# GroupNorm on one core: VectorE's loop holds one tile a trip with register addresses, and the last store is cut into quarters

## The chip, the cores and the metric

One core of one Trainium2 chip. The metric is the device time of one execution, in microseconds.

## The reference

x is (128, 1024, 32, 16) in bf16. Every batch entry has 32 groups of 32 channels; each group is normalised over its 16,384 values, then scaled and shifted by channel.

```python
def reference(x, g, b):
    G = 32
    B, C, H, W = x.shape[0], x.shape[1], x.shape[2], x.shape[3]
    xr = x.reshape(B, G, C // G, H, W)
    mu = xr.mean(axis=(2, 3, 4), keepdims=True)
    var = ((xr - mu) ** 2).mean(axis=(2, 3, 4), keepdims=True)
    xn = (xr - mu) / jnp.sqrt(var + 1e-5)
    xn = xn.reshape(B, C, H, W)
    return xn * g[None, :, None, None] + b[None, :, None, None]
```

134 MB must be read and 134 MB written.

## The kernel before

A tile is four batch entries: 128 partitions (4 entries x 32 groups), 16,384 bf16 values each, 4 MB in all. There are 32 tiles and a ring of six slots in which tiles are normalised in place. The steps of a tile:

- TensorE sums 12 chunks of 512 columns with an identity matrix. VectorE adds the other 10,240 columns in pairs (`pair`, 5120 wide, with an accumulator).
- ScalarE makes the mean of both, then two Square passes with accumulators (`ja`), variance and square root.
- VectorE makes scale and bias, and 32 passes of 128x512, one a channel.
- The store leaves when the whole tile is normalised.

One queue (SyncE) issues all loads and stores: two stores at first, then always three loads and three stores. VectorE does the pair sum of the next tile before it normalises the present one. Five trips of six unrolled tiles are a loop; the last two tiles are code behind it. In the very last tile TensorE sums all 32 chunks, so VectorE has no pair sum to do.

```python
    def on_sync(e):
        def load(j):
            if j >= SLOTS:
                e.wait_ge(st[j % SLOTS], 16 * (j // SLOTS))
            e.dma_start(out=slot(j), in_=x_v[j]).then_inc(ld[j % SLOTS], 16)

        def store(i):
            e.wait_ge(done[i % SLOTS], i // SLOTS + 1)
            e.dma_start(out=o_v[i], in_=slot(i)).then_inc(
                st[i % SLOTS] if i + SLOTS < NT else s_fin, 16
            )
        for j in range(SLOTS):
            load(j)
        for i in range(NT):
            store(i)
            if i % RUN == FIRST_RUN - 1:
                for j in range(max(SLOTS, i + 1 + SLOTS - RUN), min(i + 1 + SLOTS, NT)):
                    load(j)
        e.wait_ge(s_fin, 16 * SLOTS)

    def in_rounds(e, one):
        with nc.Fori(0, TRIPS, 1, engines=[e.engine]) as t:      # TRIPS = 5, SLOTS = 6
            for c in range(SLOTS):
                one(c, t + 1)
        for c in range(NT - LOOPED):                             # the last two tiles
            one(c, TRIPS + 1)
    # ... (cut: PE, ACT)
    def on_vector(e):
        # ... (cut)
        def one(c, turn):
            follows = not isinstance(turn, int)
            then = (c + 1) % SLOTS, turn + (c + 1) // SLOTS
            if follows:
                pair(*then)
            e.wait_ge(stded[c], turn)
            # ... (cut: reciprocal, scl, bia, each behind a semaphore)
            for k in range(KC):                                  # KC = 32
                if k == 1 and follows:
                    e.wait_ge(paired[then[0]], then[1])
                a = slot(c)[:, k * HW : (k + 1) * HW]
                ts = e.tensor_scalar(
                    out=a, in0=a, scalar1=scl[:, k : k + 1], scalar2=bia[:, k : k + 1],
                    op0=ALU.mult, op1=ALU.add,
                )
            ts.then_inc(done[c], 1)
```

Of the kernel before, what the change touches and what calls it, by code (L numbers as in the profile page):

```python
# [8 lines left out]
ALU = mybir.AluOpType  # L9
# [5 lines left out]
EPS = 1e-5  # L15

SLOTS = 6
TRIPS = 5
RUN = 3
FIRST_RUN = 2  # L20
PS_BUFS = 3
PE_CHUNKS = 12
MM_FREE = 512
# [3 lines left out]
def kernel(  # L27
# [23 lines left out]
    F = KC * HW  # L51
    inv_n = 1.0 / float(F)
    NMM = F // MM_FREE
    LOOPED = TRIPS * SLOTS
    PAIRED = F - PE_CHUNKS * MM_FREE
    assert SLOTS < NT and LOOPED < NT - 1 and NT - LOOPED <= SLOTS
    assert F % MM_FREE == 0 and PAIRED % 2 == 0 and SLOTS % PS_BUFS == 0

    x_v = x.rearrange("(t n) (g k) h w -> t (n g) (k h w)", n=NS, g=G)
# [30 lines left out]
    def sem(name):  # L90
        return nc.alloc_semaphore(name)

    def sems(name):
        return [sem(f"{name}{c}") for c in range(SLOTS)]

    ld, st, summed, paired, meaned, stded, done = (
        sems(n) for n in ("ld", "st", "sum", "pair", "mean", "std", "done")
    )

    half, both, varred, inverted, scaled, shifted = (  # L100
        sems(n) for n in ("half", "both", "var", "inv", "scl", "bia")
    )
    s_gb, s_ones, s_eye, s_gbp, s_fin = (
        sem(n) for n in ("gbl", "ones", "eye", "gbp", "fin")
    )

    def slot(i):
        return ring[:, (i % SLOTS) * F : (i % SLOTS + 1) * F]
# [4 lines left out]
    def sums_and_pairs(c):  # L113
        return ps[:, c % PS_BUFS * 2 * MM_FREE : c % PS_BUFS * 2 * MM_FREE + MM_FREE + 1]

    def pairs(c):
        return ps[:, (c % PS_BUFS * 2 + 1) * MM_FREE : (c % PS_BUFS * 2 + 1) * MM_FREE + 1]

    def on_sync(e):
        def load(j):  # L120
            if j >= SLOTS:
                e.wait_ge(st[j % SLOTS], 16 * (j // SLOTS))
            e.dma_start(out=slot(j), in_=x_v[j]).then_inc(ld[j % SLOTS], 16)  # L123

        def store(i):
            e.wait_ge(done[i % SLOTS], i // SLOTS + 1)
            e.dma_start(out=o_v[i], in_=slot(i)).then_inc(
                st[i % SLOTS] if i + SLOTS < NT else s_fin, 16
            )

        for j in range(SLOTS):
            load(j)
        for i in range(NT):
            store(i)
            if i % RUN == FIRST_RUN - 1:
                for j in range(max(SLOTS, i + 1 + SLOTS - RUN), min(i + 1 + SLOTS, NT)):
                    load(j)
        e.wait_ge(s_fin, 16 * SLOTS)

    def on_gpsimd(e):  # L140
        e.wait_ge(s_ones, 1)
        e.affine_select(  # L142
            out=eye[:], in_=ones_b[:], pattern=[[-1, P]], compare_op=ALU.is_equal,
            fill=0.0, base=0, channel_multiplier=1,
        ).then_inc(s_eye, 1)
        e.affine_select(  # L146
            out=rep[:].rearrange("q (n a) -> q n a", n=NS),
            in_=ones_b[0:G, :].rearrange("q (n a) -> q n a", n=NS),
            pattern=[[0, NS], [-1, G]], compare_op=ALU.is_equal,
            fill=0.0, base=0, channel_multiplier=1,  # L150
        ).then_inc(s_eye, 1)

    def in_rounds(e, one):

        with nc.Fori(0, TRIPS, 1, engines=[e.engine]) as t:
            for c in range(SLOTS):
                one(c, t + 1)
        for c in range(NT - LOOPED):
            one(c, TRIPS + 1)

    def is_last(c, turn):
        return isinstance(turn, int) and LOOPED + c == NT - 1

    def on_tensor(e):
        e.wait_ge(s_eye, 2)
        e.wait_ge(s_gb, 32)
        e.matmul(out=gb_p[:], lhsT=rep[:], rhs=gb_b[:], start=True, stop=True).then_inc(s_gbp, 1)  # L167
        def one(c, turn):
            e.wait_ge(meaned[(c - PS_BUFS) % SLOTS], turn)
            e.wait_ge(ld[c], turn * 16)  # L170
            chunks = NMM if is_last(c, turn) else PE_CHUNKS
            for k in range(chunks):
                mm = e.matmul(  # L173
                    out=sums(c),
                    lhsT=eye[:],
                    rhs=slot(c)[:, k * MM_FREE : (k + 1) * MM_FREE],
                    start=(k == 0),
                    stop=(k == chunks - 1),
                )
            mm.then_inc(summed[c], 1)  # L180

        in_rounds(e, one)

    def on_scalar(e):
        e.dma_start(out=gb_b[:, 0:KC], in_=g_v).then_inc(s_gb, 16)
        e.dma_start(out=gb_b[:, KC : 2 * KC], in_=b_v).then_inc(s_gb, 16)
        e.wait_ge(s_ones, 1)
        e.activation(out=warm[:], in_=eps_t[:], func=ACT.Sqrt)  # L188

        def one(c, turn):  # L190
            if not is_last(c, turn):
                e.wait_ge(paired[c], turn)
            e.wait_ge(summed[c], turn)
            src = sums(c) if is_last(c, turn) else sums_and_pairs(c)
            e.activation(  # L195
                out=jm[:, 0 : src.shape[1]], in_=src, func=ACT.Identity, scale=-inv_n,
                accum_out=nm[:, c : c + 1], saturate=False,
            ).then_inc(meaned[c], 1)
            e.wait_ge(meaned[c], turn + (1 if c >= PS_BUFS else 0))
            for h in range(2):  # L200
                if h == 1:
                    e.wait_ge(half[c], turn)
                e.activation(  # L203
                    out=ja[:],
                    in_=slot(c)[:, h * (F // 2) : (h + 1) * (F // 2)],
                    func=ACT.Square,
                    bias=nm[:, c : c + 1],
                    scale=1.0,
                    accum_out=sq[:, h : h + 1],
                    saturate=False,  # L210
                ).then_inc(both[c] if h == 1 else half[c], 1)
            e.wait_ge(both[c], turn)
            e.activation(  # L213
                out=var[:], in_=sq[:, 0:1], func=ACT.Identity, bias=eps_t[:], scale=inv_n
            ).then_inc(varred[c], 1)
            e.wait_ge(varred[c], turn)
            e.activation(  # L217
                out=std[:, c : c + 1], in_=sq[:, 1:2], func=ACT.Sqrt, bias=var[:], scale=inv_n
            ).then_inc(stded[c], 1)

        in_rounds(e, one)

    def on_vector(e):
        e.memset(ones_b[:], 1.0)  # L224
        e.memset(eps_t[:], EPS)
        e.drain()  # L226
        e.sem_inc(s_ones, 1)
        for c in range(PS_BUFS, SLOTS):
            e.sem_inc(meaned[c], 1)
        e.wait_ge(s_gbp, 1)  # L230
        e.tensor_copy(out=gb[:], in_=gb_p[:])  # L231

        def pair(c, turn):
            first, w = PE_CHUNKS * MM_FREE, PAIRED // 2
            e.wait_ge(ld[c], turn * 16)
            e.scalar_tensor_tensor(  # L236
                out=jp[:],
                in0=slot(c)[:, first : first + w],
                scalar=1.0,
                in1=slot(c)[:, first + w : first + 2 * w],  # L240
                op0=ALU.mult,
                op1=ALU.add,
                accum_out=pairs(c),
                saturate=False,
            ).then_inc(paired[c], 1)

        def one(c, turn):
            follows = not isinstance(turn, int)
            then = (c + 1) % SLOTS, turn + (c + 1) // SLOTS
            if follows:  # L250
                pair(*then)
            e.wait_ge(stded[c], turn)
            e.reciprocal(out=rstd[:], in_=std[:, c : c + 1]).then_inc(inverted[c], 1)  # L253
            e.wait_ge(inverted[c], turn)
            e.tensor_scalar(  # L255
                out=scl[:], in0=gb[:, 0:KC], scalar1=rstd[:], scalar2=None, op0=ALU.mult
            ).then_inc(scaled[c], 1)
            e.wait_ge(scaled[c], turn)
            e.scalar_tensor_tensor(  # L259
                out=bia[:], in0=scl[:], scalar=nm[:, c : c + 1], in1=gb[:, KC : 2 * KC],  # L260
                op0=ALU.mult, op1=ALU.add,
            ).then_inc(shifted[c], 1)
            e.wait_ge(shifted[c], turn)
            for k in range(KC):
                if k == 1 and follows:
                    e.wait_ge(paired[then[0]], then[1])
                a = slot(c)[:, k * HW : (k + 1) * HW]
                ts = e.tensor_scalar(  # L268
                    out=a, in0=a, scalar1=scl[:, k : k + 1], scalar2=bia[:, k : k + 1],
                    op0=ALU.mult, op1=ALU.add,  # L270
                )
            ts.then_inc(done[c], 1)

        pair(0, 1)
        e.drain()  # L275
        in_rounds(e, one)

    with tc.tile_critical(no_gpsimd_drain=True):  # L278
        on_sync(nc.sync)
# [34 lines left out]
```

## Time and profile before

| | before |
|---|---|
| time, median of 4 runs | 632.68 us (632.24 to 633.53) |
| span of the profiled execution | 630.3 us |
| moved by DMA | 268.4 MB, 433 GB/s in most slices |
| VectorE, one tile | 16.56 us (95.70 to 112.26 below) |
| ScalarE, one tile | 15.75 us (504.0 / 32) |
| DMA, load and store of one tile | 19.4 us (2 x 9.7) |

The page (the profile's summary) of the kernel before, in which PE is TensorE, PEld its weight loads, DVE VectorE, ACT ScalarE and POOL GpSimd: busy shares, then the span in 40 slices (each digit the busy share in tenths).

```profile
span 630.3 us, 2508 instructions
...
PE 157.6 (25%) x405; PEld 52.0 (8%) x405; DVE 522.3 (83%) x1185; ACT 504.0 (80%) x258; POOL 0.8 (0%) x6
...
DVE  1579999999996998599589949994997799499671
ACT  0799999999996999399859958993999399769930
...
DMA  8999999999999999999999999999999999999996
GB/s 366 433 431 416 433 433 434 430 433 435 435 435 433 430 433 433 435 433 435 433 433 428 433 433 426 433 433 437 430 433 433 433 428 433 433 433 429 433 410 285
...
```

The two bottom lines matter: the DMA engines are full from the second slice to the last but one, at 430 to 435 GB/s in most of them (410 to 437 in all), while VectorE (83%) and ScalarE (80%) have slack. The slices tell two more things: the transfers start almost at once (8 in the first slice), and something is missing in the last two (410 and 285 GB/s).

VectorE in two tiles early in the kernel (start, duration, engine, line, operation, count):

```profile
...
95.70 5.50 DVE L236 SCALAR_TENSOR_TENSOR jp<-ring 128x5120 fp8e5<-128x5120 bf16 x1
...
101.91 10.42 DVE L268 TENSOR_SCALAR ring<-ring,scl,bia 128x512 bf16<-128x512 bf16 x32
112.26 5.48 DVE L236 SCALAR_TENSOR_TENSOR jp<-ring 128x5120 fp8e5<-128x5120 bf16 x1
...
```

From one pair sum to the next are 112.26 - 95.70 = 16.56 us, with no pause.

Who VectorE waits for (total us, times, longest):

```profile
...
DVE jp L236 <- DMA ring<-in_x_dram: 63.8, 9, 8.9
...
DVE rstd L253 <- ACT std L217: 15.5, 3, 6.2
...
```

Nine waits for a load, one for every three tiles: VectorE is ahead of the transfers.

The end of the kernel before, by stretches: busy us and number of instructions of PE, PEld, DVE, ACT and POOL, then the granted TensorE clock; the two last columns are the mean busy share of the 16 DMA engines and their GB/s:

```profile
...
605.00:613.00 8.00, 0.00 (x0) 0.00 (x0) 7.76 (x25) 0.10 (x1) 0.00 (x0) 0.50 1.02 442
613.00:617.00 4.00, 0.00 (x0) 0.00 (x0) 3.33 (x11) 0.00 (x0) 0.00 (x0) 0.50 0.29 123
617.00:620.00 3.00, 0.00 (x0) 0.00 (x0) 0.00 (x0) 0.00 (x0) 0.00 (x0) 0.50 1.18 502
620.00:625.00 5.00, 0.00 (x0) 0.00 (x0) 0.00 (x0) 0.00 (x0) 0.00 (x0) 0.50 0.99 426
625.00:632.00 7.00, 0.00 (x0) 0.00 (x0) 0.00 (x0) 0.00 (x0) 0.00 (x0) 0.50 0.21 90
...
```

From 613 to 617 us the DMA engines are 29% busy: VectorE is at work on the last tile (its last pass ends at 616.3 us) and only then does its store leave. This looks like 3 us to be had. But the mean hides the engines. The trace has the times of 16 landings for each transfer (increments of its semaphore), which are read here as one from each DMA engine when its share is done. In order of time (us from the span's start, taken from the trace's landing events; first, twelfth and the last four of the 16):

```
store of the last tile but one   613.87 ... 615.49   616.65  618.01  618.87  619.41
store of the last tile           627.29 ... 627.41   627.44  627.67  628.54  629.08
```

If the last landing of each belongs to the same engine, that engine took 629.08 - 619.41 = 9.67 us for its share, as long as for the transfer before (609.74 to 619.41): it never waited for VectorE. The span ends 1.3 us after it.

### The profile page before, as it was taken

What the parts mean: (1) busy time and instruction counts of PE and PEld (TensorE: products, weight loads), DVE (VectorE), ACT (ScalarE), POOL (GpSimd) and SP (SyncE); (2) the same over time, 40 slices, a digit from 0 to 9 for tenths busy, and PEclk for the clock granted to TensorE, in tenths of its full rate; (3) what the DMA queues carried; (4) which work ended last, traced back from release to release, by engine and by line L of the source; (5) the groups of instructions that cost most, each with busy time, mean ns of one, the idle gap of its engine ahead of it and who ended that gap; (6) DMA issues with size and microseconds to landing.
All of it is one profiled execution on the core that took longest, in us unless ns stands there. A gap on an engine that the chain in (4) does not pass through costs nothing.

```text
span 630.3 us, 2508 instructions
## 1 busy us (share of the span) xinstructions
PE 157.6 (25%) x405; PEld 52.0 (8%) x405; DVE 522.3 (83%) x1185; ACT 504.0 (80%) x258; POOL 0.8 (0%) x6
## 2 busy tenths in 40 slices
PE   1453205005302320250052015203510450065000
PEld 0110001001100100010010001001100110012000
DVE  1579999999996998599589949994997799499671
ACT  0799999999996999399859958993999399769930
POOL 0000000000000000000000000000000000000000
PEclk9867656556655665665566556655665665567555
DMA  8999999999999999999999999999999999999996
GB/s 366 433 431 416 433 433 434 430 433 435 435 435 433 430 433 433 435 433 435 433 433 428 433 433 426 433 433 437 430 433 433 433 428 433 433 433 429 433 410 285
DMA packets 9316, 268.48 MB, mean 426 GB/s; under 512 B 1120, under 2 KB 1120, under 8 KB 1120
## 3 DMA queue, kind: packets, MB, share of 16 engines
q1 hardware_dynamic: 9216, 268.44, 99.0%
q8 instruction: 1, 0.02, 0.0%
q14 instruction: 3, 0.02, 0.0%
q10 hardware_dynamic: 96, 0.00, 0.0%
HBM read 134.22 MB, written 134.22 MB: 426 GB/s over the span
## 4 chain that ended last, share of the span: by engine, by line
DMA 63%; DVE 26%; ACT 7%; issue 0%; SPq 0%; DVEq 0%
DMA out_dram<-ring 43%; DMA ring<-in_x_dram 20%; DVE ring L268 16%; DVE jp L236 9%; ACT ja L203 7%; DVE bia L259 0%; DVE scl L255 0%; ACT jm L195 0%; SPq L123 0%; ACT var L213 0%; DVE rstd L253 0%; ACT std L217 0%; DVEq L275 0%; SPq L309 0%; SPq L278 0%
## 5 line engine op out<-in xcount | busy, mean ns | idle before, releaser
L203 ACT ACTIVATE ja<-ring,nm 128x8192 fp8e5<-128x8192 bf16 x64 | 455.9, 7123 | 2.1
L268 DVE TENSOR_SCALAR ring<-ring,scl,bia 128x512 bf16<-128x512 bf16 x1024 | 333.7, 408 | 1.2
L173 PE MATMUL ps<-ring,eye 128*128 128x512 bf16 x404 | 157.4, 571 | 411.8 <-DMA ring<-in_x_dram 411.8
L236 DVE SCALAR_TENSOR_TENSOR jp<-ring 128x5120 fp8e5<-128x5120 bf16 x31 | 170.1, 5488 | 63.8 <-DMA ring<-in_x_dram 63.8
L195 ACT ACTIVATE jm<-ps 128x513 fp8e5<-128x513 f32 (+1 forms) x32 | 19.2, 601 | 95.0 <-DVE jp L236 95.0
L173 PEld LDWEIGHTS ps<-ring,eye 128*128 128x128 bf16 x404 | 51.9, 134 | 516.9 <-issue 467.2
L253 DVE RECIPROCAL rstd<-std 128x1 f32<-128x1 f32 x32 | 6.3, 198 | 15.5 <-ACT std L217 15.5
L203 ACT ACTIVATION_READ_ACCUMULATOR ja<-ring,nm 128x1 f32 x64 | 12.0, 187 | 0.0
L217 ACT ACTIVATE std<-sq,var 128x1 f32<-128x1 f32 x32 | 9.4, 295 | 1.0
L213 ACT ACTIVATE var<-sq,eps_t 128x1 f32<-128x1 f32 x32 | 9.4, 295 | 1.0
L259 DVE SCALAR_TENSOR_TENSOR bia<-scl,nm,gb 128x32 f32<-128x32 f32 x32 | 8.0, 251 | 1.1
L255 DVE TENSOR_SCALAR scl<-gb,rstd 128x32 f32<-128x32 f32 x32 | 7.7, 241 | 1.1
L231 DVE COPY gb<-gb_p 128x64 f32<-128x64 f32 x1 | 0.2, 225 | 10.1 <-PE gb_p L167 10.1
L195 ACT ACTIVATION_READ_ACCUMULATOR jm<-ps 128x1 f32 x32 | 6.2, 194 | 0.0
L236 DVE DVE_READ_ACCUMULATOR jp<-ring 128x1 f32 x31 | 4.4, 143 | 0.0
L167 PE MATMUL gb_p<-gb_b,rep 32*128 32x64 bf16 x1 | 0.2, 205 | 11.2 <-DMA gb_b<-in_b_dram 11.2
L188 ACT ACT_TABLE_LOAD x1 | 1.3, 1283 | 1.9 <-issue 1.9
L224 DVE MEMSET ones_b<- 128x128 bf16 x1 | 0.2, 165 | 1.1 <-SPq L278 1.1
L167 PEld LDWEIGHTS gb_p<-gb_b,rep 32*128 32x128 bf16 x1 | 0.1, 100 | 11.1 <-issue 11.1
L146 POOL TENSOR_SCALAR_AFFINE_SELECT rep<-ones_b 32x128 bf16<-32x128 bf16 x1 | 0.3, 304 | 0.0
L142 POOL TENSOR_SCALAR_AFFINE_SELECT eye<-ones_b 128x128 bf16<-128x128 bf16 x1 | 0.3, 295 | 0.9 <-DVEq L226 0.9
L188 ACT ACTIVATE warm<-eps_t 128x1 f32<-128x1 f32 x1 | 0.2, 203 | 0.0
(5 smaller groups left out, 0.5 us busy)
## 6 DMA issues: line engine op xcount, KB each, us to landing
ring<-in_x_dram SPq DMA_DIRECT2D x32, 4096.0 KB, 29.1
out_dram<-ring SPq DMA_DIRECT2D x32, 4096.0 KB, 33.9
gb_b<-in_g_dram ACTq DMA_DIRECT2D x1, 2.0 KB, 6.4
gb_b<-in_b_dram ACTq DMA_DIRECT2D x1, 2.0 KB, 9.6
```

What stands on the lines that cost most here:

```text
L167: e.matmul(out=gb_p[:], lhsT=rep[:], rhs=gb_b[:], start=True, stop=True).then_inc(s_gbp, 1)
L173: mm = e.matmul(out=sums(c), lhsT=eye[:], rhs=slot(c)[:, k * MM_FREE : (k + 1) * MM_FREE], start=(k == 0), stop=(k == chunks - 1),)
L188: e.activation(out=warm[:], in_=eps_t[:], func=ACT.Sqrt)
L195: e.activation(out=jm[:, 0 : src.shape[1]], in_=src, func=ACT.Identity, scale=-inv_n, accum_out=nm[:, c : c + 1], saturate=False,).then_in ...
L203: e.activation(out=ja[:], in_=slot(c)[:, h * (F // 2) : (h + 1) * (F // 2)], func=ACT.Square, bias=nm[:, c : c + 1], scale=1.0, accum_out= ...
L213: e.activation(out=var[:], in_=sq[:, 0:1], func=ACT.Identity, bias=eps_t[:], scale=inv_n).then_inc(varred[c], 1)
L217: e.activation(out=std[:, c : c + 1], in_=sq[:, 1:2], func=ACT.Sqrt, bias=var[:], scale=inv_n).then_inc(stded[c], 1)
L236: e.scalar_tensor_tensor(out=jp[:], in0=slot(c)[:, first : first + w], scalar=1.0, in1=slot(c)[:, first + w : first + 2 * w], op0=ALU.mult ...
L253: e.reciprocal(out=rstd[:], in_=std[:, c : c + 1]).then_inc(inverted[c], 1)
L255: e.tensor_scalar(out=scl[:], in0=gb[:, 0:KC], scalar1=rstd[:], scalar2=None, op0=ALU.mult).then_inc(scaled[c], 1)
L259: e.scalar_tensor_tensor(out=bia[:], in0=scl[:], scalar=nm[:, c : c + 1], in1=gb[:, KC : 2 * KC], op0=ALU.mult, op1=ALU.add,).then_inc(shi ...
L268: ts = e.tensor_scalar(out=a, in0=a, scalar1=scl[:, k : k + 1], scalar2=bia[:, k : k + 1], op0=ALU.mult, op1=ALU.add,)
```

## The change

Its intent: VectorE's code shrinks to a loop of one tile a trip (one round of the loop). The tile's addresses are computed in registers ahead of use, while the pair sum runs, and held there; no code follows the loops; and the last tile is stored in four column quarters, each as soon as its eight channels are normalised. To avoid separate code for the last tile, VectorE does its pair sum as well. Two orders change with it: VectorE's pair sum waits for TensorE's first matmul on the tile instead of the load itself, and TensorE's last chunk waits for the pair sum, so that ScalarE waits for one semaphore.

```diff
 def on_sync(e):
+            w = F // store_parts(i)                     # 4 parts for the last tile, else 1
+            for p in range(store_parts(i)):
+                e.wait_ge(done, NQ * i + NQ // store_parts(i) * (p + 1))
+                e.dma_start(
+                    out=o_v[i][:, p * w : (p + 1) * w], in_=slot(i)[:, p * w : (p + 1) * w]
+                ).then_inc(st[i % SLOTS] if i + SLOTS < NT else s_fin, 16)
 ... (cut)
 def on_tensor(e):
-            chunks = NMM if is_last(c, turn) else PE_CHUNKS
+                elif k == PE_CHUNKS - 1:
+                    e.wait_ge(paired, t * SLOTS + (c + 1))
 ... (cut)
+                if k == 0:
+                    mm.then_inc(first_in, 1)
 ... (cut: ScalarE's waits; the loops of PE and ACT; initial memsets move to GpSimd)
 def on_vector(e):
+        with nc.Fori(0, NT, 1, engines=[e.engine]) as i:
+            with e.If(i < NT - 1):
+                e.drain()
+                pair(i + 1)                             # waits for first_in
+            parts = [part(i, k * HW, HW) for k in range(KC)]
+            e.keepalive_nop([e.lower_ap(a) for a in parts])
+            e.wait_ge(stded, i + 1)
+            e.reciprocal(out=rstd[:], in_=std[:, bass.ds(i % SLOTS, 1)]).then_inc(inverted, 1)
 ... (cut: scl, bia)
+            for k, a in enumerate(parts):
                 ts = e.tensor_scalar(
                     out=a, in0=a, scalar1=scl[:, k : k + 1], scalar2=bia[:, k : k + 1],
                     op0=ALU.mult, op1=ALU.add,
                 )
-            ts.then_inc(done[c], 1)
+                if (k + 1) % KQ == 0:                   # after 8, 16, 24, 32 channels
+                    ts.then_inc(done, 1)
```

More of the change, by code (lines that the diff above doesn't have):

```diff
@@ L17 @@
 SLOTS = 6
-TRIPS = 5
-RUN = 3
-FIRST_RUN = 2
+RUNS = (2, 3, 3, 3, 3, 3, 3, 3, 3, 6)
+NQ = 4
 PS_BUFS = 3
@@ L53 @@
     NMM = F // MM_FREE
-    LOOPED = TRIPS * SLOTS
+    ROUNDS = -(-NT // SLOTS)
+    REST = NT - (ROUNDS - 1) * SLOTS
+    KQ = KC // NQ
     PAIRED = F - PE_CHUNKS * MM_FREE
-    assert SLOTS < NT and LOOPED < NT - 1 and NT - LOOPED <= SLOTS
+    ITEM = 2
+    assert NT > SLOTS and 0 < REST < SLOTS and sum(RUNS) == NT and RUNS[-1] == SLOTS
     assert F % MM_FREE == 0 and PAIRED % 2 == 0 and SLOTS % PS_BUFS == 0
@@ L94, in sems @@
         return [sem(f"{name}{c}") for c in range(SLOTS)]
-    ld, st, summed, paired, meaned, stded, done = (
-        sems(n) for n in ("ld", "st", "sum", "pair", "mean", "std", "done")
-    )
-    half, both, varred, inverted, scaled, shifted = (
-        sems(n) for n in ("half", "both", "var", "inv", "scl", "bia")
-    )
+    ld, st, summed, meaned = (sems(n) for n in ("ld", "st", "sum", "mean"))
+    half, both, varred = (sems(n) for n in ("half", "both", "var"))
+    inverted, scaled, shifted = (sem(n) for n in ("inv", "scl", "bia"))
+    first_in, paired, stded, done = (sem(n) for n in ("first", "pair", "std", "done"))
     s_gb, s_ones, s_eye, s_gbp, s_fin = (
@@ L105, with store_parts @@
     )
+    def store_parts(i):
+        return NQ if i == NT - 1 else 1
     def slot(i):
@@ L114, in sums_and_pairs @@
         return ps[:, c % PS_BUFS * 2 * MM_FREE : c % PS_BUFS * 2 * MM_FREE + MM_FREE + 1]
-    def pairs(c):
-        return ps[:, (c % PS_BUFS * 2 + 1) * MM_FREE : (c % PS_BUFS * 2 + 1) * MM_FREE + 1]
     def on_sync(e):
@@ L125, in store @@
         def store(i):
-            e.wait_ge(done[i % SLOTS], i // SLOTS + 1)
-            e.dma_start(out=o_v[i], in_=slot(i)).then_inc(
-                st[i % SLOTS] if i + SLOTS < NT else s_fin, 16
-            )
+            w = F // store_parts(i)
[4 more added lines that the diff above has]
+                ).then_inc(st[i % SLOTS] if i + SLOTS < NT else s_fin, 16)
         for j in range(SLOTS):
             load(j)
-        for i in range(NT):
-            store(i)
-            if i % RUN == FIRST_RUN - 1:
-                for j in range(max(SLOTS, i + 1 + SLOTS - RUN), min(i + 1 + SLOTS, NT)):
-                    load(j)
-        e.wait_ge(s_fin, 16 * SLOTS)
-    def on_gpsimd(e):
-        e.wait_ge(s_ones, 1)
+        i = 0
+        for run in RUNS:
+            for n in range(run):
+                store(i + n)
+            i += run
+            for j in range(i + SLOTS - run, min(i + SLOTS, NT)):
+                load(j)
+        e.wait_ge(s_fin, 16 * sum(store_parts(i) for i in range(NT - SLOTS, NT)))
+    def on_gpsimd(e):
+        e.memset(ones_b[:], 1.0)
+        e.memset(eps_t[:], EPS)
+        e.drain()
+        e.sem_inc(s_ones, 1)
+        for c in range(SLOTS - 2, SLOTS):
+            e.sem_inc(meaned[c], 1)
         e.affine_select(
@@ L153, in in_rounds @@
     def in_rounds(e, one):
-        with nc.Fori(0, TRIPS, 1, engines=[e.engine]) as t:
-            for c in range(SLOTS):
-                one(c, t + 1)
-        for c in range(NT - LOOPED):
-            one(c, TRIPS + 1)
-    def is_last(c, turn):
-        return isinstance(turn, int) and LOOPED + c == NT - 1
+        with nc.Fori(0, ROUNDS, 1, engines=[e.engine]) as t:
+            for c in range(REST):
+                one(c, t)
+            with e.If(t < ROUNDS - 1):
+                for c in range(REST, SLOTS):
+                    one(c, t)
     def on_tensor(e):
@@ L167, in on_tensor, with one @@
         e.matmul(out=gb_p[:], lhsT=rep[:], rhs=gb_b[:], start=True, stop=True).then_inc(s_gbp, 1)
-        def one(c, turn):
-            e.wait_ge(meaned[(c - PS_BUFS) % SLOTS], turn)
-            e.wait_ge(ld[c], turn * 16)
-            chunks = NMM if is_last(c, turn) else PE_CHUNKS
-            for k in range(chunks):
+        def one(c, t):
+            for k in range(PE_CHUNKS):
+                if k == 0:
+                    e.wait_ge(ld[c], (t + 1) * 16)
+                elif k == PE_CHUNKS - 2:
+                    e.wait_ge(meaned[(c - 2) % SLOTS], t + 1)
+                elif k == PE_CHUNKS - 1:
+                    e.wait_ge(paired, t * SLOTS + (c + 1))
                 mm = e.matmul(
@@ L177, in one @@
                     start=(k == 0),
-                    stop=(k == chunks - 1),
+                    stop=(k == PE_CHUNKS - 1),
                 )
+                if k == 0:
+                    mm.then_inc(first_in, 1)
             mm.then_inc(summed[c], 1)
@@ L188, in on_scalar, with one @@
         e.activation(out=warm[:], in_=eps_t[:], func=ACT.Sqrt)
-        def one(c, turn):
-            if not is_last(c, turn):
-                e.wait_ge(paired[c], turn)
-            e.wait_ge(summed[c], turn)
-            src = sums(c) if is_last(c, turn) else sums_and_pairs(c)
+        def one(c, t):
+            e.wait_ge(summed[c], t + 1)
             e.activation(
-                out=jm[:, 0 : src.shape[1]], in_=src, func=ACT.Identity, scale=-inv_n,
+                out=jm[:], in_=sums_and_pairs(c), func=ACT.Identity, scale=-inv_n,
                 accum_out=nm[:, c : c + 1], saturate=False,
             ).then_inc(meaned[c], 1)
-            e.wait_ge(meaned[c], turn + (1 if c >= PS_BUFS else 0))
-            for h in range(2):
-                if h == 1:
-                    e.wait_ge(half[c], turn)
+            for h, (ready, at) in enumerate(
+                ((meaned[c], t + (2 if c >= SLOTS - 2 else 1)), (half[c], t + 1))
+            ):
+                e.wait_ge(ready, at)
                 e.activation(
@@ L210, in one @@
                     saturate=False,
-                ).then_inc(both[c] if h == 1 else half[c], 1)
-            e.wait_ge(both[c], turn)
+                ).then_inc((half, both)[h][c], 1)
+            e.wait_ge(both[c], t + 1)
             e.activation(
@@ L215, in one @@
             ).then_inc(varred[c], 1)
-            e.wait_ge(varred[c], turn)
+            e.wait_ge(varred[c], t + 1)
             e.activation(
                 out=std[:, c : c + 1], in_=sq[:, 1:2], func=ACT.Sqrt, bias=var[:], scale=inv_n
-            ).then_inc(stded[c], 1)
+            ).then_inc(stded, 1)
         in_rounds(e, one)
     def on_vector(e):
-        e.memset(ones_b[:], 1.0)
-        e.memset(eps_t[:], EPS)
-        e.drain()
-        e.sem_inc(s_ones, 1)
-        for c in range(PS_BUFS, SLOTS):
-            e.sem_inc(meaned[c], 1)
+        bytes_of_ring = ring[:].bitcast(mybir.dt.uint8)
@@ new lines, in part, with pair @@
+        def part(i, lo, n):
+            at = (i % SLOTS) * (F * ITEM) + lo * ITEM
+            return bytes_of_ring[:, bass.ds(at, n * ITEM)].bitcast(BF16)
+        def pair(i):
+            lo, n = PE_CHUNKS * MM_FREE, PAIRED // 2
+            e.wait_ge(first_in, i + 1)
+            e.scalar_tensor_tensor(
+                out=jp[:],
+                in0=part(i, lo, n),
+                scalar=1.0,
+                in1=part(i, lo + n, n),
+                op0=ALU.mult,
+                op1=ALU.add,
+                accum_out=ps[:, bass.ds((i % PS_BUFS) * (2 * MM_FREE) + MM_FREE, 1)],
+                saturate=False,
+            ).then_inc(paired, 1)
@@ L230, in on_vector @@
         e.wait_ge(s_gbp, 1)
         e.tensor_copy(out=gb[:], in_=gb_p[:])
-        def pair(c, turn):
-            first, w = PE_CHUNKS * MM_FREE, PAIRED // 2
-            e.wait_ge(ld[c], turn * 16)
-            e.scalar_tensor_tensor(
-                out=jp[:],
-                in0=slot(c)[:, first : first + w],
-                scalar=1.0,
-                in1=slot(c)[:, first + w : first + 2 * w],
-                op0=ALU.mult,
-                op1=ALU.add,
-                accum_out=pairs(c),
-                saturate=False,
-            ).then_inc(paired[c], 1)
@@ L247, in one @@
-        def one(c, turn):
-            follows = not isinstance(turn, int)
-            then = (c + 1) % SLOTS, turn + (c + 1) // SLOTS
-            if follows:
-                pair(*then)
-            e.wait_ge(stded[c], turn)
-            e.reciprocal(out=rstd[:], in_=std[:, c : c + 1]).then_inc(inverted[c], 1)
-            e.wait_ge(inverted[c], turn)
+        pair(0)
+        with nc.Fori(0, NT, 1, engines=[e.engine]) as i:
+            with e.If(i < NT - 1):
+                e.drain()
+                pair(i + 1)
[3 more added lines that the diff above has]
+            e.reciprocal(out=rstd[:], in_=std[:, bass.ds(i % SLOTS, 1)]).then_inc(inverted, 1)
+            e.wait_ge(inverted, i + 1)
@@ L255, in one @@
             e.tensor_scalar(
                 out=scl[:], in0=gb[:, 0:KC], scalar1=rstd[:], scalar2=None, op0=ALU.mult
-            ).then_inc(scaled[c], 1)
-            e.wait_ge(scaled[c], turn)
+            ).then_inc(scaled, 1)
+            e.wait_ge(scaled, i + 1)
             e.scalar_tensor_tensor(
-                out=bia[:], in0=scl[:], scalar=nm[:, c : c + 1], in1=gb[:, KC : 2 * KC],
-                op0=ALU.mult, op1=ALU.add,
-            ).then_inc(shifted[c], 1)
-            e.wait_ge(shifted[c], turn)
@@ L264, in one @@
-            for k in range(KC):
-                if k == 1 and follows:
-                    e.wait_ge(paired[then[0]], then[1])
-                a = slot(c)[:, k * HW : (k + 1) * HW]
+                out=bia[:], in0=scl[:], scalar=nm[:, bass.ds(i % SLOTS, 1)],
+                in1=gb[:, KC : 2 * KC], op0=ALU.mult, op1=ALU.add,
+            ).then_inc(shifted, 1)
+            e.wait_ge(shifted, i + 1)
+            for k, a in enumerate(parts):
                 ts = e.tensor_scalar(
@@ L271, in one @@
                 )
-            ts.then_inc(done[c], 1)
-        pair(0, 1)
-        e.drain()
-        in_rounds(e, one)
+                if (k + 1) % KQ == 0:
+                    ts.then_inc(done, 1)
     with tc.tile_critical(no_gpsimd_drain=True):
```

## The prediction

(Its landing times are on a clock 0.3 us later than the one used in the rest of this document. The forecast came to 632.3 us, 0.5 below the 632.77 it starts from. The 1.0 us a tile is the author's estimate, as are 0.6 and 0.2 to 0.3 us, two of its terms. What the trace of before shows of it: VectorE's register operations lasted 40 to 63 ns, a record that came directly behind one started 0.07 to 0.09 us after its start, and the register operation behind the back edge's two started 0.35 to 0.42 us after the first of them.)

> **What bounds it now.** The transfers. The page's slices show DMA busy at 0.9 or more and about 433 GB/s from the second slice to the last but two. 268.44 MB at 433 GB/s are 620 of the 630.3 us of the span. [...] One 4 MB transfer takes about 9.7 us, a load and a store 19.4 to 19.5 us per tile. VectorE needs 16.55 us per tile (chain of waits: 35.70 to 52.25), ScalarE 15.75 us (504.0/32). In steady state VectorE idles 5 to 9 us for a load in every three tiles (view of waits: 63.8 us in 9), and each store is issued some 20 us before the queue has run dry, because loads and stores lie two transfers deep in one queue.
>
> **What the change costs.** VectorE, per tile: a back edge and a compare-branch (in this trace 40 + 56 ns, next instruction 0.3 us after the first), a drain, and address arithmetic behind it (a fused register operation takes 46 to 63 ns[...]). Behind the drain 3 or 4 of these are bare, about 0.6 us; the address of the mean column, behind a semaphore, 0.2 to 0.3 us; the 32 addresses of a tile should hide under the pair sum (5.5 us) unless each needs three separate operations. Estimate: 1.0 us per tile, so about 17.6 us, still under 19.5. The pair sum also starts after the first matmul instead of after the load (+0.5 us), and ScalarE's mean after a last matmul behind the pair sum (+0.5 us); both off the critical path. Early, VectorE is busy without a pause to 112 us; the stores of tiles 1 and 4 have about 8 to 9 us to spare there, and I expect 5 us of it used.
>
> **The tail.** The last tile's pair sum returns to VectorE (5.5 us in a gap of 4.8 us), so the last normalise ends about 620 instead of 616.3 us. In the stretch from 613.5 to 617 us most DMA engines idle, waiting for the last store; with quarters they would not. Taken alone that suggests a gain of 3.5 us. But the landing events show that the 16 engines have drifted apart: the store before the last lands from 614.2 us (first engine) to 619.7 us (last engine), the last store from 627.6 to 629.4. The slowest engine goes from 619.71 to 629.38, that is 9.67 us, one full transfer: it never waited. It ends the kernel, and quarters give it no less to do[...]. The fast engines will finish earlier, for nothing. So I expect almost none of the 3.5 us.
>
> **Prediction.** 632.3 us against 632.77, 8 in 10 between 629.8 and 634.5. Faster by over 2%: 0.01; within 2%: 0.95; slower by over 2%: 0.04.
>
> **What would show it.** DMA still about 433 GB/s in the middle slices; no stretch in which the DMA engines idle before 605 us; VectorE at 17 to 18.5 us per tile with shorter idle waits for loads; the fast engines' last landing about 3 us earlier, the slowest within 1 us of 629.4; the last normalise ending later than before.
>
> **What would make it wrong.** If the addresses are not hidden under the pair sum and VectorE exceeds 19.5 us per tile, it becomes the bound, at once 32 times the excess. At 18.5 us per tile or more the early stores of tiles 1 and 4 come late and a few us are lost once. If the drift of the engines is weaker without the profiler, quarters give up to 3.5 us (0.6%).

## The result, and the profile after

| | before | after |
|---|---|---|
| time, median of 4 runs | 632.68 us (632.24 to 633.53) | 632.74 us (632.52 to 632.82) |
| span of the profiled execution | 630.3 us | 631.1 us |
| VectorE, one tile | 16.56 us | 17.23 us |
| VectorE's last pass ends | 616.3 us | 620.6 us |
| last landing, first / last DMA engine | 627.29 / 629.08 us | 624.72 / 629.69 us |

The ratio of the times is 0.9999, with a 95% interval of 0.9981 to 1.0016: the same. Here and below a ratio is the mean time of one kernel's fast runs over that of the other's of the same rounds, so it is not quite the ratio of the medians quoted.

The same lines of the page, after:

```profile
span 631.1 us, 2973 instructions
...
PE 158.2 (25%) x380; PEld 49.9 (8%) x385; DVE 529.4 (84%) x1185; ACT 504.0 (80%) x258; POOL 1.0 (0%) x8
...
DVE  1579999999999999699689959995998699599963
ACT  0798999999999999699948977894999499859960
...
DMA  8999999999999999999999999999999999999996
GB/s 366 432 432 413 434 434 430 438 432 432 432 432 432 430 432 432 434 430 434 432 432 428 432 432 430 432 432 432 426 432 432 432 434 432 434 434 434 438 410 263
...
```

The transfers are unchanged: full, at 432 to 434 GB/s in most slices (410 to 438 from the second to the last but one).

The same stretch of VectorE:

```profile
...
99.53 5.49 DVE L243 SCALAR_TENSOR_TENSOR jp<-ring 128x5120 fp8e5 x1 [0.50 <-issue]
...
105.84 10.43 DVE L276 TENSOR_SCALAR ring<-ring,scl,bia  x32
116.76 5.49 DVE L243 SCALAR_TENSOR_TENSOR jp<-ring 128x5120 fp8e5 x1 [0.50 <-issue]
```

116.76 - 99.53 = 17.23 us, 0.67 more than before. "[0.50 <-issue]" says where most of it is: VectorE stands still for 0.50 us before the pair sum and waits for no other engine. This is the drain (its record runs from 95.58 to 99.08 us and the last pass ends at 99.04, so the pair sum no longer starts 0.07 us before that, as it did before: 101.91 + 10.42 against 112.26) and the register arithmetic behind it. The rest was read from this run's own trace, which has a record for each of VectorE's register instructions (duration in ns, of the tile that begins at 99.08 us):

```
 40 ALU_OP, 130 and 115 FUSED_REGOPS     between drain and pair sum
131, 100, 100, 93, 93, 76 FUSED_REGOPS   the 32 addresses, while the pair sum runs: 0.8 us with their gaps
 40 ALU_OP, 53 FUSED_REGOPS              address of the standard deviation, still under the pair sum
 40 ALU_OP                               address of the mean, between scl and bia
 40 ALU_OP, 56 COMPARE_BRANCH, 36 MOVE, 50 COMPARE_BRANCH
                                         the back edge and the branch round the drain, while passes run
```

In the whole trace of this run VectorE's fused register instructions lasted 53 to 136 ns and its compare-and-branches 47 to 63 ns.

The waits after:

```profile
...
DVE jp L243 <- PE ps L184: 49.4, 8, 7.8
DVE jp L243 <- issue: 12.0, 24, 0.5
DVE rstd L264 <- ACT std L227: 11.9, 2, 6.4
...
```

The wait for loads is now read as one for TensorE's first matmul (49.4 us, with 12.0 us of issue), and is shorter than 63.8: VectorE gave up some slack and still waits.

The end of the kernel after:

```profile
...
605.00:613.00 8.00, 0.00 (x0) 0.00 (x0) 3.52 (x12) 4.08 (x4) 0.00 (x0) 0.50 0.95 410
613.00:617.00 4.00, 0.00 (x0) 0.00 (x0) 4.00 (x14) 0.00 (x0) 0.00 (x0) 0.50 1.00 420
617.00:620.00 3.00, 0.00 (x0) 0.00 (x0) 3.00 (x11) 0.00 (x0) 0.00 (x0) 0.50 0.93 388
620.00:625.00 5.00, 0.00 (x0) 0.00 (x0) 0.56 (x2) 0.00 (x0) 0.00 (x0) 0.50 0.93 388
625.00:632.00 7.00, 0.00 (x0) 0.00 (x0) 0.00 (x0) 0.00 (x0) 0.00 (x0) 0.50 0.12 50
...
```

The hole from 613 to 617 us is closed (1.00 instead of 0.29), although VectorE ends 4.3 us later than before. The last stretch is emptier: 11 of the 16 DMA engines are done by 624.9 us. The slowest still lands at 629.69. (The landings of the four quarters overlap in time; they are told apart here and below by following each engine from quarter to quarter, about 2.45 us apart.)

VectorE ends later, but it is not itself what is late: before its last normalise it waits 5.50 us for ScalarE's statistics (4.54 before). ScalarE has them 4.04 us later, because its mean now waits for TensorE's last matmul and so for VectorE's pair sum: 1.40 us for each of the last two tiles, against 0.71 and nothing before, and the two means are 17.23 us apart instead of 15.74.

### The profile page after: what moved, and what is told of

The parts are those of the page before. It is cut to its first block, busy times and chain, and to the rows that moved or that the text cites. A ratio compares the mean times of both kernels' runs of the same rounds, so it can differ in the third digit from the quotient of the medians.

```text
span 631.1 us, 2973 instructions
## 1 busy us (share of the span) xinstructions
PE 158.2 (25%) x380; PEld 49.9 (8%) x385; DVE 529.4 (84%) x1185; ACT 504.0 (80%) x258; POOL 1.0 (0%) x8
## 4 chain that ended last, share of the span: by engine, by line
ACT 50%; DMA 34%; DVE 6%; issue 5%; PE 2%; DVEq 2%; SPq 0%
ACT ja L213 46%; DMA out_dram<-ring 18%; DMA ring<-in_x_dram 16%; DVE ring L276 5%; PE ps L184 2%; ACT jm L205 2%; DVEq L259 1%; ACT var L223 1%; ACT std L227 1%; DVE jp L243 1%; DVEq L262 0%; DVEq L264 0%; DVE bia L270 0%; DVE scl L266 0%; DVEq L243 0%
## 5 line engine op out<-in xcount | busy, mean ns | idle before, releaser
L276 DVE TENSOR_SCALAR ring<-ring,scl,bia x1024 | 333.5, 405 | 1.2
L243 DVE SCALAR_TENSOR_TENSOR jp<-ring 128x5120 fp8e5 (+1 forms) x32 | 175.7, 5492 | 61.4 <-PE ps L184 49.4
L205 ACT ACTIVATE jm<-ps 128x513 fp8e5<-128x513 f32 x32 | 19.3, 602 | 99.0 <-PE ps L184 99.0
L184 PEld LDWEIGHTS ps<-ring,eye 128*128 128x128 bf16 x384 | 49.8, 137 | 531.8 <-DVE jp L243 313.5
L264 DVE RECIPROCAL rstd<-std 128x1 f32 x32 | 6.3, 196 | 11.9 <-ACT std L227 11.9
L243 DVE DVE_READ_ACCUMULATOR jp<-ring (+1 forms) x32 | 4.5, 140 | 0.0
## 6 DMA issues: line engine op xcount, KB each, us to landing
out_dram<-ring SPq DMA_DIRECT2D x31, 4096.0 KB, 31.5
```

Of the source, the lines that this page charges most:

```text
L184: mm = e.matmul(out=sums(c), lhsT=eye[:], rhs=slot(c)[:, k * MM_FREE : (k + 1) * MM_FREE], start=(k == 0), stop=(k == PE_CHUNKS - 1),)
L205: e.activation(out=jm[:], in_=sums_and_pairs(c), func=ACT.Identity, scale=-inv_n, accum_out=nm[:, c : c + 1], saturate=False,).then_inc(me ...
L243: e.scalar_tensor_tensor(out=jp[:], in0=part(i, lo, n), scalar=1.0, in1=part(i, lo + n, n), op0=ALU.mult, op1=ALU.add, accum_out=ps[:, bas ...
L264: e.reciprocal(out=rstd[:], in_=std[:, bass.ds(i % SLOTS, 1)]).then_inc(inverted, 1)
L276: ts = e.tensor_scalar(out=a, in0=a, scalar1=scl[:, k : k + 1], scalar2=bia[:, k : k + 1], op0=ALU.mult, op1=ALU.add,)
```

## The experiments

Theory A: the kernel ends when the slowest DMA engine has moved its sixteenth of 268 MB; it never waits in either kernel, so neither VectorE's longer trip nor the quarters reach the end. The rivals: the hole before the last store is lost time (B; B names another claim in the second run), the later end is paid in full (C), something other than the transfers is the floor (D), VectorE's trip already sets the pace (E), and the deep queue hides even a far longer trip (F).

### Quarters alone

The kernel before with only the last store cut up.

```diff
 def store(i):
-            e.wait_ge(done[i % SLOTS], i // SLOTS + 1)
-            e.dma_start(out=o_v[i], in_=slot(i)).then_inc(
-                st[i % SLOTS] if i + SLOTS < NT else s_fin, 16
-            )
+            parts = NQ if i == NT - 1 else 1
+            w = F // parts
+            for p in range(parts):
+                e.wait_ge(done[i % SLOTS], i // SLOTS + 1 + p)
+                e.dma_start(
+                    out=o_v[i][:, p * w : (p + 1) * w], in_=slot(i)[:, p * w : (p + 1) * w]
+                ).then_inc(st[i % SLOTS] if i + SLOTS < NT else s_fin, 16)
 ... (cut: the final wait; VectorE reports each quarter of the last tile)
```

> The kernel before, with only the last store cut into four column quarters, each issued when its eight channels are normalised. Theory A (the slowest DMA engine ends the kernel and never waits for the last store): the fast engines' last landing moves from 627.6 to about 624 us, the slowest stays at 629 to 630, time within 0.5 us of before (632.2 to 633.3). Rival B (the 3.5 us in which most DMA engines idle before the last store are lost to the kernel): 3 to 3.5 us faster, about 629.3.

Measured: 633.15 us (5 runs, 632.82 to 633.72) against 632.73 (11 runs of before on the same chip), ratio 1.0004 (0.9991 to 1.0017). Its end by stretches:

```profile
...
613.00:617.00 4.00, 0.00 (x0) 0.00 (x0) 4.00 (x13) 0.00 (x0) 0.00 (x0) 0.50 0.90 381
617.00:620.00 3.00, 0.00 (x0) 0.00 (x0) 0.51 (x2) 0.00 (x0) 0.00 (x0) 0.50 0.98 415
620.00:625.00 5.00, 0.00 (x0) 0.00 (x0) 0.00 (x0) 0.00 (x0) 0.00 (x0) 0.50 0.80 336
625.00:632.00 7.00, 0.00 (x0) 0.00 (x0) 0.00 (x0) 0.00 (x0) 0.00 (x0) 0.50 0.07 29
...
```

The hole is gone (0.90 against 0.29), the fast engines land from 623.8 instead of 627.3 us, and the time has not moved. The slowest landing is at 630.48 us. B falls: the hole was in engines that did not end the kernel.

### The loop with one last store

The kernel after, with the last tile stored in one piece.

```diff
     def store_parts(i):
-        return NQ if i == NT - 1 else 1
+        return 1
```

> The kernel after, with the last tile stored in one piece. Its last normalise ends at 620.6 us, 4.3 later than before. Theory A: now all engines, the slowest too, wait for the one store, so all land about 4.5 us after the fast engines of before did (627.3 + 4.5 = 631.8 to 632), 1.5 to 2 us later than the slowest of after: time 634.2 to 634.8, +0.25%. Rival B (quarters buy nothing whatever the end): 632.7 as after. Rival C (the loop's later end is paid in full): 637.

Measured: 634.36 us (5 runs, 634.01 to 634.67), ratio to before 1.0023 (1.0011 to 1.0036): slower by 0.2%, which is clear of noise. Its end:

```profile
...
613.00:617.00 4.00, 0.00 (x0) 0.00 (x0) 4.00 (x14) 0.00 (x0) 0.00 (x0) 0.50 0.19 82
617.00:620.00 3.00, 0.00 (x0) 0.00 (x0) 3.00 (x11) 0.00 (x0) 0.00 (x0) 0.50 0.03 11
620.00:625.00 5.00, 0.00 (x0) 0.00 (x0) 0.23 (x1) 0.00 (x0) 0.00 (x0) 0.50 0.98 419
625.00:632.00 7.00, 0.00 (x0) 0.00 (x0) 0.00 (x0) 0.00 (x0) 0.00 (x0) 0.50 0.70 300
...
```

The hole now lasts to 620 us (0.19 and 0.03), and all 16 engines land within 0.2 us, from 631.18 to 631.38. The slowest landed its share of the store before at 619.54, and 11.84 us later the last one. It had needed 9.77 for each of the transfers before, so about 2.1 us were waiting. So the quarters are worth about 1.6 us in this kernel (634.36 - 632.74; the two were timed in different rounds, in which before took 632.73 and 632.68), though nothing in the kernel before. The rivals of this run, that quarters buy nothing whatever the end (632.7) and that the later end is paid in full (637), both miss; A's 634.2 to 634.8 holds.

### Transfers alone

Wrong result: the kernel before without any compute; a store waits for its load.

```diff
 def store(i):
-            e.wait_ge(done[i % SLOTS], i // SLOTS + 1)
+            e.wait_ge(ld[i % SLOTS], 16 * (i // SLOTS + 1))
 ... (cut: GpSimd, TensorE, ScalarE and VectorE programs taken out)
```

> Wrong result on purpose: the same loads and stores in the same order on the same queue, each store waiting for its load alone, no compute at all. It shows the floor. Theory A (transfers bound everything, and the drift between DMA engines is theirs): the spread of the last landings stays 4 to 6 us, time 631 to 633. Rival D (the compute engines' memory traffic slows some DMA engines, or waits hide in the middle): the spread shrinks to 1 us or less, time about 626 or lower.

Measured: 631.04 us (6 runs, 629.63 to 632.22), ratio to before 0.9972 (0.9959 to 0.9984). The landings of the last store spread from 623.92 to 628.04, 4.1 us.

```profile
span 629.1 us, 111 instructions
...
DMA  8999999999999999999999999999999999999996
GB/s 367 433 433 413 433 433 433 433 433 433 421 433 433 433 433 433 433 431 433 433 433 431 433 433 427 433 433 433 431 433 433 433 433 433 433 425 431 433 433 290
...
```

The DMA lines are those of the real kernels. The kernel before takes 1.7 us more than this floor (632.73 - 631.04), so better timed compute around the same transfers can win about 0.3% (0.2 to 0.4% by the interval). D falls: there is no hidden loss of several us in the middle, and the DMA engines drift apart without any compute. The drift was somewhat smaller here: at the store of the last tile but two, the 16 landings spread over 4.1 and 3.3 us in the two runs without compute (this one and a probe below), and over 4.9 to 6.7 us in six with it (before, after, and four of these experiments; the run with eighteen passes more, which the transfers do not bound, is left out). Compute may add to it, but with so few runs this is not settled.

### Six passes more in VectorE's trip

The kernel after, with six passes more over the first channels (x times one plus zero: the result stays right).

```diff
+            for a in parts[0:EXTRA]:                    # EXTRA = 6
+                ts = e.tensor_scalar(
+                    out=a, in0=a, scalar1=1.0, scalar2=0.0, op0=ALU.mult, op1=ALU.add,
+                )
+            ts.then_inc(twice, 1)
+            e.wait_ge(twice, i + 1)
             for k, a in enumerate(parts):
```

> The kernel after, with six more 128x512 passes (times one, plus zero, right result) in VectorE's trip: about 2.0 us more a tile, 19.3 us, just under the 19.4 to 19.5 us of a tile's transfers. Theory A: no lasting bound; the early store of tile 4 comes 10 us later with 2 us to spare, so about 8 us are lost once, and the end comes 0 to 4 us later: 640 to 645. Rival E (VectorE's trip already sets the pace and its 0.7 us of loop overhead were paid for by something else): +2.0 x 32 = 698.

Measured: 637.43 us (4 runs, 637.07 to 637.72), ratio 1.0071 (1.0056 to 1.0086). Slower than after by 4.7 us, not by 32 times anything: E falls. The range expected was too high because the passes were cheaper than assumed: the trip grew by 1.34 us, from 17.23 to 18.57, not by 2.0 (a pass with constant scalars started every 0.20 us, one with per-partition scalars every 0.32). The loss is where A put it, once, around the store of tile 4:

```profile
...
110.00:115.00 5.00, 4.53 (x11) 1.60 (x12) 4.76 (x19) 3.85 (x3) 0.00 (x0) 0.50 0.99 426
115.00:120.00 5.00, 0.81 (x2) 0.00 (x0) 5.00 (x17) 4.97 (x3) 0.00 (x0) 0.84 0.94 406
120.00:125.00 5.00, 0.00 (x0) 0.00 (x0) 4.50 (x11) 5.00 (x1) 0.00 (x0) 0.50 0.26 111
125.00:130.00 5.00, 0.95 (x3) 0.41 (x4) 4.80 (x7) 2.20 (x5) 0.00 (x0) 0.50 1.15 492
...
```

Between 120 and 125 us the DMA engines fall to 0.26. That store was issued at 122.96 us here, at 116.30 in the kernel after and at 112.36 before. The 6.66 us of delay against after moved its landing by 4.2 us, so after had 2.5 us to spare there and before 6.4. In the kernel after the same stretches are full:

```profile
...
115.00:120.00 5.00, 0.00 (x0) 0.00 (x0) 4.50 (x5) 5.00 (x1) 0.00 (x0) 0.50 1.03 446
120.00:125.00 5.00, 2.62 (x7) 0.97 (x8) 4.80 (x11) 3.51 (x7) 0.00 (x0) 0.50 1.03 446
...
```

### Eighteen passes more

The run above with eighteen passes in place of six.

```diff
-EXTRA = 6
+EXTRA = 18
```

> As extra6, with 18 more passes: six of them lengthened a tile's trip from 17.23 to 18.57 us, so 18 should give about 21.1 us, above the 19.5 us of a tile's transfers. Theory A: now VectorE sets the pace; first normalise at 37 us, 30 trips of 21.1 us, then ScalarE's last statistics, the last normalise and the last quarter, about 35 us: span about 706 us, time 700 to 713. Rival F (the deep queue of transfers hides it): below 650.

Measured: 705.58 us (one run). VectorE's trip is 21.01 us (from pair sum to pair sum, 345.68 to 366.69).

```profile
span 703.9 us, 3549 instructions
...
DVE  2499999999999999999999999999999999999986
...
DMA  9999999399989989998998999899989989997438
...
```

VectorE is at 9 from the third slice to the last but two and the DMA digits break up into 8 and 9 with holes. The transfers of a tile take 19.4 us, the trip 21.0: the bound has moved to VectorE. The threshold lies between the two doses, as A says; F falls.

### Which DMA engines are late, without compute

Wrong result: transfers alone, with 15 tiny loads of 1 to 15 partitions behind the last store. In this run a load of n partitions gave n landings, besides one early write to its semaphore. They are read here as one from each of n DMA engines, those of a smaller load being among those of a larger one; the run does not show this by itself. Read so, the difference between n and n+1 shows one engine, and the twelfth engine, say, is the one that joins with 12 partitions.

```diff
+        for n in range(1, 16):
+            e.dma_start(
+                out=probe[0:n, 64 * n : 64 * (n + 1)], in_=x_v[0][0:n, 64 * n : 64 * (n + 1)]
+            ).then_inc(arrived[n], 16)
         e.wait_ge(s_fin, 16 * SLOTS)
```

> Wrong result on purpose: dma_only with 15 tiny loads of 1 to 15 partitions queued behind the last store, each with its own semaphore. [...] Theory A: the same nested order is seen in all 15, two to four engines are 1.5 to 5 us later than the others. If late engines are different from one tiny load to the next, the drift is not the engines' own.

Measured: 630.69 us (one run). The last store landed at 623.81 to 624.99 us on 14 engines, and at 627.05 and 627.08 on two. A late landing (627.22, the next latest 626.50) first shows in the tiny load of 12 partitions, and there is still only one in that of 15: read as above, the two late engines are the twelfth and one that took no tiny load, the sixteenth, both about 2.6 us behind the median.

### Which DMA engines are late, in the kernel after

```diff
+            if i == NT - 1:
+                for p, n in enumerate(PROBES):          # 3, 4, 7, 8, 11, 12, 15
+                    e.dma_start(
+                        out=probe[0:n, 32 * p : 32 * (p + 1)],
+                        in_=x_v[0][0:n, 32 * p : 32 * (p + 1)],
+                    ).then_inc(arrived[p], 16)
             w = F // store_parts(i)
```

> The kernel after, with seven tiny loads (of 3, 4, 7, 8, 11, 12 and 15 partitions) queued between the store of the last tile but one and the last store: the landing times show which DMA engines are behind at that moment. If the late ones are fixed engines and those of the probe without compute: the 12th and the 16th again, perhaps the 4th and the 8th with them, 2 to 6 us behind; all others within 1 us. If lateness is not tied to an engine, others show. Time within 1 us of after (632 to 633.5).

Measured: 632.68 us (one run), correct. The load of 4 partitions landed by 614.78 us, that of 7 at 619.29, and up to 12 no second late one came; by 15 another did (617.78). So, on the same reading, the latest engine was one of the fifth to seventh, 5 us behind, another one of the thirteenth to fifteenth, and the twelfth was on time. A third share of the store before the probes landed at 616.18, 1.8 us behind the median, and its engine took no tiny load (the load of 15 had landed by 615.73 on all but the two late engines): it is the sixteenth. The last quarter then landed at 627.40 and 629.62 on two engines and by 625.98 on the others. The expectation that the same engines are always late fell for the twelfth; the sixteenth was behind in both probes, by 2.6 and 1.8 us. The two probes ran on different chips, so lateness may belong to a chip's engines or to the execution; this stays open. On one chip, at the store of the last tile but two, two engines were more than 2.2 us behind the median with quarters alone, and one each in the loop with one store, with six passes more and with transfers alone; at 1.8 us it is four with transfers alone. That speaks against a set that is wholly fixed for a chip, but is no proof.

## Why the prediction was right

- **The transfers bound it.** Right. The flat 433 GB/s stayed, and transfers alone take 631.04 us.
- **VectorE's loop costs about 1.0 us a tile, off the path.** The mechanism was right, the size too high: 0.67 us, of it 0.50 before the pair sum (0.6 forecast), 0.1 before the bias (its 32 instructions were preceded by 4.2 us of idle time, 1.1 before; 0.2 to 0.3 each forecast), and 0.07 of lost overlap at the drain. The back edge, which the forecast named too, lies under the passes and costs nothing that shows (32 passes take 10.43 us with it, 10.42 without). The 32 addresses hide under the pair sum easily: six fused register instructions, 0.8 us of 5.5. Extra passes showed the edge: at 18.57 us a tile a few us are lost once, at 21.01 the loop is the bound.
- **The early stores have 8 to 9 us to spare, 5 will be used.** 4 us were used (issue of tile 4's store 112.36 to 116.30), but only 6.4 us were there. The forecast took the landing of the transfer ahead as the limit. The time around the transfer has to be taken off: with six passes more this store met nearly idle DMA engines, and 11.4 us passed from its issue to its first landing (122.96 to 134.37), 1.7 more than the 9.7 of a transfer. The margin left is 2.5 us.
- **The quarters gain nothing because the slowest DMA engine never waits.** Right for the kernel before, shown by the quarters alone (1.0004). The extra completions cost little: from the landing of the last tile but two to the end, the slowest engine took 19.34 us before (609.74 to 629.08) and 19.58 after (610.11 to 629.69); there it had already needed 9.76 for the transfer before (600.35 to 610.11), so at most 0.1 us is left for them.
- **The last normalise ends about 620 us.** Right in number (620.6), but the path named, a pair sum too long for VectorE's gap, is not what set it: VectorE still waited 5.50 us for ScalarE, whose mean had been held up by the pair sum through TensorE. From the end of the pair sum's accumulator read to ScalarE's mean it was 0.04 us before (573.50 to 573.54) and 0.70 after (592.60 to 593.30); the forecast had this as 0.5 and off the critical path, and here it is on the path to the last store.
- **The fast engines finish earlier, for nothing.** This step was incomplete. The prediction itself put the last normalise 4 us later and did not ask what one whole store would do then. The run without quarters answers: all 16 engines would have waited for it and the kernel would have been 1.6 us slower. The quarters bought back what the one-tile loop with the last pair sum on VectorE, and the new order of waits, would have cost; no run separates these. The net of zero is thus one small loss and one equal gain, besides everything that stays hidden.

The best version measured is a tie of before and after; nothing here beats them beyond noise, and transfers alone leave 0.3%.

## What to carry to other kernels

Look at the landings of the single DMA engines before you value a hole in the mean DMA share, and see which engine ends the kernel. Here a hole in the engines that did not end the kernel was filled (0.29 to 0.90 by the quarters alone) and the time stayed (ratio 1.0004), while about 2.1 us of waiting in the engine that ended last cost about 1.6 us (the loop with one last store). When a change moves two ends at once, ask what each would do without the other; a tie can be a loss and a gain of equal size. The register arithmetic for a whole tile's 32 addresses, 0.8 us, hid under one instruction of 5.5 us, and a queue of transfers (in the kernel after a store landed 31.5 us after its issue in the median, against 9.7 for one transfer) hid a trip that grew to 17.23 us; at 18.57 it lost 4.7 us once, early, and at 21.01, above the 19.4 of the transfers, it lost time in every trip.
